# Sign of the float64 weights: from a ScalarE pass over one byte to a VectorE operation on the high word

## Chip, cores and metric

One core of a Trainium2 chip runs the whole program. The metric is the device time of that core in microseconds, as the median of several executions; a profiled execution is one more, with a span from its first to its last instruction.

## What is computed

Attention in which every query keeps its 32 best keys, over 8 batches x 8 heads x 576 positions x 64 dimensions, followed by a two-layer feed-forward block with an ELU between the layers, on 4608 tokens of width 512 and a hidden width of 2048:

```python
scores = scale * np.matmul(q, k.transpose(0, 1, 3, 2))
kth = np.partition(scores, -top_k, axis=-1)[..., -top_k:-top_k + 1]
scores = np.where(scores >= kth, scores, -1000000000.0)
scores = scores - np.max(scores, axis=-1, keepdims=True)
attn = np.exp(scores)
attn = attn / (np.sum(attn, axis=-1, keepdims=True) + 1e-09)
x = np.matmul(attn, v)          # (B,H,S,D) -> (B*S, H*D)
...
h = x @ w_in
g = np.where(h > 0.0, h, alpha * (np.exp(np.minimum(h, 0.0)) - 1.0))
out = g @ w_out
```

`q`, `k` and `v` arrive as float32. `w_in` and `w_out` arrive as float64, because the scaling of the random numbers promotes them; the kernel sees them as pairs of 32-bit words and turns them into float32 itself.

## The kernel before

**Steps.** The attention is cut into 144 steps. A step is 128 queries (a query tile, or the remainder rows) of a pair of heads. In a step TensorE computes scores for a step two ahead (L299) and ScalarE copies them out of PSUM (L307). VectorE finds the 32 best of each of 2 x 576 scores: it takes the 8 greatest (MAX8) and replaces them (MATCH_REPLACE8), four times and three times. GpSimd makes two small biases from the least and the greatest of the kept (L366, L368), ScalarE masks with a steep Prelu and takes the exponential (L369, L370), GpSimd normalises (L380 to L387), TensorE transposes (L406), ScalarE copies (L407), TensorE multiplies with `v` (L432), and ScalarE copies the result into `xT` (L459).

**Feed-forward pieces.** When all tiles of a block of tokens are in `xT`, its feed-forward work is cut into pieces: `hidden` (TensorE L504, ScalarE Relu twice and Exp, L514 to L519) and `project` (TensorE L529). `feed` puts pieces between attention work so that the total is spread evenly over the steps; a piece is held back until the weights that it needs count as decoded (`decoded`). The last operation of the activation function, a "gate" (L476), runs on VectorE: one operation with two tensors in, of 128x512 or 128x768.

**Who sets the order.** In the first eight steps (`n < tight`) a scheduler of the framework places the instructions of all engines, and `select_row` works row by row. From step 8 on the order is that of the program (`manual_schedule`), and `select` works on both rows at once. Each engine takes its instructions strictly in its order. Loads are issued on SyncE's queue.

**Weight decoding.** The weights come in 32 pieces of 128 x 512 numbers, 16 of `w_in` and 16 of `w_out`. `hook` is called after two of each row's passes and runs one `decode_piece` each time: four in one of the first eight steps, the last three in step 8. `load_weight` fetches a piece into a `raw` tile of 128 x 1024 words; seven such tiles take turns. In a `raw` tile the low and the high words alternate, so each is read with a stride of 8 bytes. `convert_first` works on three fields in place. ScalarE turns the low word into a small number that holds the lower mantissa bits (Copy, L174), turns one byte of the high word into a sign (Sign, L175, written as an 8-bit float into the top byte of the low word), and takes the scaled magnitude of the high word (Abs, L178). GpSimd clamps that magnitude (L179). Three pieces later `convert_last` shifts the high word left by three bits on VectorE (L186), and GpSimd adds the high and the low word as integers into the final tile, `w_in` or `w_out` (L187), which brings sign, exponent and mantissa together.

Of the kernel before, what the change touches and what calls it, by code (L numbers as in the profile page):

```python
# [8 lines left out]
AF = mybir.ActivationFunctionType  # L9
ALU = mybir.AluOpType  # L10
FP32 = mybir.dt.float32
U32 = mybir.dt.uint32
I32 = mybir.dt.int32
FP8 = mybir.dt.float8e4
PSUM = bass.MemoryType.PSUM

TOP_K = 32
# [64 lines left out]
def kernel(  # L82
# [9 lines left out]
    nc = tc.nc  # L92
# [9 lines left out]
    NF = dff // P  # L102
# [3 lines left out]
    scale = 1.0 / float(D) ** 0.5  # L106
# [33 lines left out]
    raw = {}  # L140

    def weight(i):
        per = dff // WN
        if i < NC * per:
            f, c = divmod(i, NC)
            src = moe_w_in[c * P : (c + 1) * P, 2 * f * WN : 2 * (f + 1) * WN]
            return src, w_in[:, c, f * WN : (f + 1) * WN]
        f = i - NC * per
        return moe_w_out[f * P : (f + 1) * P, :], w_out[:, f, :]

    def load_weight(i):
        t = rawpool.tile([P, 2 * WN], U32, tag="raw", name="raw")
        nc.sync.dma_start(t[:], weight(i)[0])
        raw[i] = t

    def parts(t):
        words = t[:].rearrange("p (n w) -> p n w", w=2)
        signs = t[:].bitcast(FP8).rearrange("p (n w) -> p n w", w=8)
        return words[:, :, 0], words[:, :, 1], signs[:, :, 3]

    def convert_first(i):

        lo, hi, sign = parts(raw[i])
        ef, mf = hi.bitcast(FP32), lo.bitcast(FP32)
        nc.scalar.activation(mf, lo, AF.Copy, scale=2.0**-35, bias=2.0**17)  # L174
        nc.scalar.activation(  # L175
            sign, ef, AF.Sign, scale=2.0**64, bias=1.0, saturate=False
        )
        nc.scalar.activation(ef, ef, AF.Abs, scale=2.0**-62)  # L178
        nc.gpsimd.tensor_scalar(  # L179
            ef, ef, (2.0 - 2.0**-3 - 2.0**-23) * 2.0**-46, 2.0**-77, ALU.min, ALU.max  # L180
        )

    def convert_last(i):
        t, dst = raw.pop(i), weight(i)[1]
        lo, hi, sign = parts(t)
        nc.vector.tensor_single_scalar(hi, hi, 3, ALU.logical_shift_left)  # L186
        nc.gpsimd.tensor_tensor(  # L187
            dst.bitcast(I32), hi.bitcast(I32), lo.bitcast(I32), ALU.add
        )

    decode = []
    decoded = [0]
# [10 lines left out]
            late["x"] = ctx.enter_context(tc.tile_pool(name="xt", bufs=2))  # L203

    def decode_piece(i):
        if i < 2 * NF:
            if i + 3 < 2 * NF:
                load_weight(i + 3)
            convert_first(i)
        if i > 2:  # L210
            convert_last(i - 3)
            decoded[0] = i - 2

    loaded, kqT, vT = {}, {}, {}

# [200 lines left out]
    def attend(g):  # L416
# [28 lines left out]
        while tiles:  # L445
            blk, lo, parts = tiles[0].block, tiles[0].cols.start, 0
            while tiles and tiles[0].block is blk:
                parts += 1
                hi = tiles.pop(0).cols.stop
            finish(blk, parts, g.hp, slice(lo, hi), ps[:, c0 : c0 + hi - lo])  # L450
            c0 += hi - lo
# [106 lines left out]
    for b in range(B):  # L558
# [12 lines left out]
        for qt in range(J + 1):  # L571
# [8 lines left out]
            t = Tile(b, qt, rows, blk, slice(c0, c0 + n))  # L580
# [6 lines left out]
        for qts in order:  # L587
# [3 lines left out]
            for qt in qts:  # L591
                n = len(steps)
# [54 lines left out]
    for hp in range(1, NHP):  # L647
        load_v(0, hp)
    decode += [lambda i=i: decode_piece(i) for i in range(2 * NF + 3)]
    at(0, start_qk, 0, 2)  # L650
    at(1, start_qk, 0, 3)
# [93 lines left out]
```

## Time and profile before

| quantity | value |
|---|---|
| median of 3 runs | 1667.17 us (1666.97 to 1669.18) |
| profiled execution | 1667.02 us, span 1665.2 us |
| TensorE matmul busy | 1592.8 us (96% of the span) |
| VectorE busy | 1495.8 us (90%) |
| ScalarE busy | 1165.1 us (70%) |
| GpSimd busy | 630.5 us (38%) |
| Copy on the low word, L174 | 32 x, 651 / 708 / 857 ns least, median, most |
| Sign into one byte, L175 | 32 x, 1327 / 1402 / 1589 ns |
| Abs on the high word, L178 | 32 x, 639 / 724 / 922 ns |
| clamp on GpSimd, L179 | 32 x, 638 / 658 / 923 ns |
| shift on VectorE, L186 | 32 x, 401 / 429 / 1281 ns |
| addition on GpSimd, L187 | 16 + 16 x, median 1038 and 1037 ns |
| gate on VectorE, L476 | 132 x, 660 / 692 / 1370 ns |

Durations of single instructions overlap: two MAX8 of some 0.75 us each are listed as 1.41 us together. What an instruction adds to a full engine is the time from its start to the start of the next. The decoding runs from 8.7 us (first Copy) to 148.6 us (start of the last addition); the rest of the span has none. A number in brackets at the end of a timeline row is the time for which the engine stood idle before it, with the instruction that ended the wait.

### The profile page before, as it was taken

What the parts mean: (1) busy time and instruction counts of PE and PEld (TensorE: products, weight loads), DVE (VectorE), ACT (ScalarE), POOL (GpSimd) and SP (SyncE); (2) the same over time, 40 slices, a digit from 0 to 9 for tenths busy, and PEclk for the clock granted to TensorE, in tenths of its full rate; (3) what the DMA queues carried; (4) which work ended last, traced back from release to release, by engine and by line L of the source; (5) the groups of instructions that cost most, each with busy time, mean ns of one, the idle gap of its engine ahead of it and who ended that gap; (6) DMA issues with size and microseconds to landing.
All of it is one profiled execution on the core that took longest, in us unless ns stands there. A gap on an engine that the chain in (4) does not pass through costs nothing.

```text
span 1665.2 us, 25986 instructions
## 1 busy us (share of the span) xinstructions
PE 1592.8 (96%) x8528; PEld 1031.5 (62%) x8528; DVE 1495.8 (90%) x3044; ACT 1165.1 (70%) x2377; POOL 630.5 (38%) x1719
## 2 busy tenths in 40 slices
PE   5589999999999999999999999999999999999999
PEld 3366677657574767656566676755557575755565
DVE  5887999999999999999999999999999999998500
ACT  6998777668686777678667685868758585857521
POOL 3775444333334334333334333333333343332200
PEclk9578999999999999999999999999999999999999
DMA  7540120001100110001100111001200100000000
GB/s 211 171 144 7 23 50 29 7 15 44 48 1 8 43 42 22 1 28 37 42 14 1 50 29 35 1 14 43 50 13 1 28 15 29 7 7 7 7 13 13
DMA packets 101126, 56.21 MB, mean 34 GB/s; under 512 B 84096, under 2 KB 92288, under 8 KB 100992
## 3 DMA queue, kind: packets, MB, share of 16 engines
q1 hardware_dynamic: 99792, 54.26, 11.7%
q8 instruction: 68, 1.11, 0.3%
q14 instruction: 66, 0.54, 0.1%
q10 hardware_dynamic: 1200, 0.30, 0.1%
HBM read 45.09 MB, written 9.44 MB: 33 GB/s over the span
## 4 chain that ended last, share of the span: by engine, by line
PE 65%; DVE 21%; ACT 9%; POOL 3%; issue 2%; SPq 0%; DMA 0%; ACTq 0%; POOLq 0%; DVEq 0%
PE ops L529 24%; PE hps L504 20%; DVE wk L346 9%; DVE m L353 8%; PE avps L432 7%; PE scps L299 6%; PE eps L406 5%; DVE m L341 3%; ACT sc L370 2%; ACT sc L369 1%; DVE gT L476 1%; ACT raw L175 1%; PE qkps L269 1%; ACT et L407 1%; POOL w_in L187 1%
## 5 line engine op out<-in xcount | busy, mean ns | idle before, releaser
L353 DVE MAX8 m<-wk 128x8 f32<-128x576 f32 x816 | 577.0, 750 | 0.0
L504 PE MATMUL hps<-xT,w_in 128*128 128x256 f32 (+2 forms) x2432 | 548.1, 374 | 12.5 <-ACT xT L459 12.3
L529 PE MATMUL ops<-w_out,gT 128*128 128x512 f32 x1152 | 522.8, 598 | 0.0
L504 PEld LDWEIGHTS hps<-xT,w_in 128*128 128x128 f32 x2432 | 406.5, 193 | 109.2 <-issue 23.8
L346 DVE MATCH_REPLACE8 wk<-m,wk 128x576 f32<-128x576 f32 x544 | 400.8, 746 | 0.0
L529 PEld LDWEIGHTS ops<-w_out,gT 128*128 128x128 f32 x1152 | 208.7, 190 | 233.0 <-issue 219.5
L380 POOL TENSOR_SCALAR dene<-den 128x2 f32<-128x2 f32 x144 | 35.9, 249 | 771.2 <-ACT sc L370 770.6
L369 ACT ACTIVATE sc<-sc,neg 128x576 f32<-128x576 f32 x288 | 226.8, 788 | 89.2 <-POOL neg L366 89.0
L370 ACT ACTIVATE sc<-sc,gap 128x576 f32<-128x576 f32 x288 | 224.1, 778 | 25.7 <-ACT sc L369 0.7
L387 POOL TENSOR_SCALAR sc<-sc,rec 128x576 f32<-128x576 f32 x288 | 221.0, 778 | 14.9
L307 ACT ACTIVATE sc<-scps 128x576 f32<-128x576 f32 x288 | 174.0, 659 | 73.3 <-PE scps L299 73.3
L299 PE MATMUL scps<-kqT 64*128 64x288 f32 (+1 forms) x1280 | 201.8, 440 | 21.2 <-ACT kqT L275 7.9
L407 ACT COPY et<-eps 128x512 f32<-128x512 f32 x288 | 166.8, 579 | 55.2 <-PE eps L406 55.0
L346 DVE MATCH_REPLACE8 wk<-m,sc 128x576 f32<-128x576 f32 x272 | 200.4, 746 | 0.0
L432 PE MATMUL avps<-et,vT 128*64 128x256 f32 (+2 forms) x2080 | 193.3, 326 | 4.8 <-ACT et L407 4.6
L406 PEld LDWEIGHTS eps<-ident,sc 128*128 128x128 f32 x1152 | 143.6, 144 | 83.8 <-issue 46.2
L476 DVE SCALAR_TENSOR_TENSOR gT<-n,gT 128x512 f32<-128x512 f32 (+1 forms) x132 | 100.2, 759 | 102.0 <-ACT n L519 101.9
L341 DVE MAX8 m<-sc 128x8 f32<-128x576 f32 x272 | 191.8, 748 | 0.0
L406 PE MATMUL eps<-ident,sc 128*128 128x128 f32 x1152 | 175.7, 278 | 15.4 <-POOL sc L387 13.0
L432 PEld LDWEIGHTS avps<-et,vT 128*64 128x64 f32 x2080 | 122.6, 141 | 79.1 <-issue 22.8
L299 PEld LDWEIGHTS scps<-kqT 64*128 64x128 f32 (+1 forms) x1280 | 108.1, 181 | 91.9 <-issue 44.2
L514 ACT ACTIVATE n<-hps 128x512 f32<-128x512 f32 (+1 forms) x156 | 88.0, 564 | 71.4 <-PE hps L504 67.5
(47 smaller groups left out, 1170.2 us busy)
## 6 DMA issues: line engine op xcount, KB each, us to landing
kin<-in_k_dram SPq DMA_DIRECT2D x64, 128.0 KB, 2.8
raw<-in_moe_w_in_dram SPq DMA_DIRECT2D x16, 512.0 KB, 5.4
vT<-in_v_dram SPq DMA_DIRECT2D x64, 128.0 KB, 2.3
raw<-in_moe_w_out_dram SPq DMA_DIRECT2D x16, 512.0 KB, 3.9
out_dram<-osb SPq DMA_DIRECT2D x32, 256.0 KB, 2.3
qin<-in_q_dram SPq DMA_DIRECT2D x62, 128.0 KB, 2.8
kin<-in_k_dram SPq DMA_DIRECT2D x32, 32.0 KB, 2.4
vT<-in_v_dram SPq DMA_DIRECT2D x64, 16.0 KB, 2.2
```

The costliest lines, as they stand in the source:

```text
L299: nc.tensor.matmul(wide[i][rows, half, 0:HS], kq[part, q0 : q0 + u.t.ql], kq[part, k0 : k0 + HS], start=True, stop=True,)
L341: nc.vector.max(found[i], cur[i])
L346: nc.vector.match_replace(wk[i], found[i], cur[i], TAKEN)
L353: nc.vector.max(found[i], cur[i])
L369: nc.scalar.activation(sc, sc, AF.Prelu, bias=neg[:], alpha=STEEP)
L370: nc.scalar.activation(sc, sc, AF.Exp, bias=gap[:], accum_out=u.den[:, i : i + 1])
L387: nc.gpsimd.tensor_scalar(u.sc[:, i, :], u.sc[:, i, :], rec[:, i : i + 1], 1.0, ALU.mult, ALU.mult)
L406: nc.tensor.transpose(ps[:, c * P : (c + 1) * P], sc[:, c0 : c0 + P], ident[:])
L407: nc.scalar.copy(g.et[:, chunks, u.at, :], ps[:, 0 : n * P].rearrange("p (c q) -> p c q", c=n),)
L432: nc.tensor.matmul(ps[i * D : (i + 1) * D, cols], vt[:, 2 * J + i if c == J else i * J + c, :], w, start=(c == 0), stop=(c == J),)
L504: nc.tensor.matmul(blk.h[:, f % bank, :], w_in[:, i, f * P : (f + 1) * P], blk.xT[:, i, 0:n_tok], start=(i == 0), stop=(i == NC - 1),)
L529: nc.tensor.matmul(blk.o[:], blk.gT[f // NG][:, f % NG, s * P : (s + 1) * P], w_out[:, f, :], start=(f == 0), stop=(f == NF - 1),)
```

## The change

The sign is no longer made by ScalarE. Abs writes the magnitude of the high word straight into the final tile, with another scale, and goes ahead of Copy. The clamp on GpSimd and the shift on VectorE work on the final tile in place. A new VectorE operation takes the sign bit of the untouched high word (AND with the top bit) and joins it (XOR) to the shifted magnitude. GpSimd's addition then adds the low word to the final tile. The four parts of a piece are issued in four successive calls of `decode_piece`: Abs and Copy at once, the clamp one call later, shift and sign two calls later, the addition three calls later. The number of calls, the number of loads and the count in `decoded` are as before.

```diff
@@ def parts(t):
         words = t[:].rearrange("p (n w) -> p n w", w=2)
-        signs = t[:].bitcast(FP8).rearrange("p (n w) -> p n w", w=8)
-        return words[:, :, 0], words[:, :, 1], signs[:, :, 3]
+        return words[:, :, 0], words[:, :, 1]
@@ def convert_first(i):
-        lo, hi, sign = parts(raw[i])
-        ef, mf = hi.bitcast(FP32), lo.bitcast(FP32)
-        nc.scalar.activation(mf, lo, AF.Copy, scale=2.0**-35, bias=2.0**17)
-        nc.scalar.activation(
-            sign, ef, AF.Sign, scale=2.0**64, bias=1.0, saturate=False
-        )
-        nc.scalar.activation(ef, ef, AF.Abs, scale=2.0**-62)
-        nc.gpsimd.tensor_scalar(
-            ef, ef, (2.0 - 2.0**-3 - 2.0**-23) * 2.0**-46, 2.0**-77, ALU.min, ALU.max
+        lo, hi = parts(raw[i])
+        nc.scalar.activation(weight(i)[1], hi.bitcast(FP32), AF.Abs, scale=2.0**-66)
+        nc.scalar.activation(lo.bitcast(FP32), lo, AF.Copy, scale=2.0**-35, bias=2.0**17)
+
+    def convert_second(i):
+        w = weight(i)[1]
+        nc.gpsimd.tensor_scalar(
+            w, w, (2.0 - 2.0**-3 - 2.0**-23) * 2.0**-50, 2.0**-81, ALU.min, ALU.max
         )
+
+    def convert_third(i):
+        w = weight(i)[1].bitcast(U32)
+        nc.vector.tensor_single_scalar(w, w, 3, ALU.logical_shift_left)
+        nc.vector.scalar_tensor_tensor(
+            out=w, in0=parts(raw[i])[1], scalar=1 << 31, in1=w,
+            op0=ALU.bitwise_and, op1=ALU.bitwise_xor,
+        )
@@ def convert_last(i):
-        t, dst = raw.pop(i), weight(i)[1]
-        lo, hi, sign = parts(t)
-        nc.vector.tensor_single_scalar(hi, hi, 3, ALU.logical_shift_left)
-        nc.gpsimd.tensor_tensor(
-            dst.bitcast(I32), hi.bitcast(I32), lo.bitcast(I32), ALU.add
-        )
+        w, t = weight(i)[1].bitcast(I32), raw.pop(i)
+        nc.gpsimd.tensor_tensor(w, w, parts(t)[0].bitcast(I32), ALU.add)
@@ def decode_piece(i):
-        if i < 2 * NF:
-            if i + 3 < 2 * NF:
-                load_weight(i + 3)
-            convert_first(i)
-        if i > 2:
-            convert_last(i - 3)
-            decoded[0] = i - 2
+        stages = (convert_first, convert_second, convert_third, convert_last)
+        if i + 3 < 2 * NF:
+            load_weight(i + 3)
+        for ago, stage in enumerate(stages):
+            if 0 <= i - ago < 2 * NF:
+                stage(i - ago)
+        decoded[0] = max(0, i - 2)
```

More of the change, by code (lines that the diff above doesn't have):

```diff
@@ L13 @@
 I32 = mybir.dt.int32
-FP8 = mybir.dt.float8e4
 PSUM = bass.MemoryType.PSUM
```

## The prediction

> **What bounds the kernel now.** I read the chain that ended last first, then the engines by stage, then the order of work on ScalarE and VectorE inside the first stage, since the edit touches nothing after it (the last shift of a weight piece, L186, starts at 148.1 us). The chain by engine, from the page:
>
> ```profile
> PE 65%; DVE 21%; ACT 9%; POOL 3%; issue 2%; SPq 0%; DMA 0%; ACTq 0%; POOLq 0%; DVEq 0%
> ```
>
> ACT's 9% (some 150 us) matters here. The stages, columns as PE, PEld, DVE, ACT, POOL busy us with counts, clock granted to PE, DMA share, GB/s:
>
> ```profile
> 52.00:67.00 15.00, 9.90 (x40) 7.20 (x41) 12.06 (x26) 14.30 (x26) 11.21 (x20) 0.50 0.62 177
> ...
> 127.00:142.00 15.00, 10.88 (x65) 8.18 (x64) 5.02 (x11) 15.00 (x28) 7.84 (x13) 0.74 0.01 2
> 150.00:200.00 50.00, 49.47 (x371) 36.26 (x370) 50.00 (x103) 38.34 (x81) 23.45 (x65) 1.00 0.07 18
> ...
> 400.00:800.00 400.00, 392.29 (x2075) 251.49 (x2072) 400.00 (x816) 291.79 (x610) 152.72 (x442) 1.00 0.10 27
> ```
>
> While weights are decoded ScalarE is full and VectorE has gaps; from 150 us on VectorE is full without a gap and TensorE nearly so. So what the edit is worth is how much earlier or later VectorE, and TensorE with it, enters that full stretch. One step (one pair of attention rows) of ScalarE's timeline:
>
> ```profile
> 51.80 0.24 ACT L459 COPY xT<-avps 128x128 f32<-128x128 f32 x1
> ...
> 59.78 1.28 ACT L174 ACTIVATE raw<-raw 128x512 f32<-128x512 uint32 x2
> 60.90 2.53 ACT L175 ACTIVATE raw<-raw 128x512 fp8e4<-128x512 f32 x2
> 63.12 1.29 ACT L178 ACTIVATE raw<-raw 128x512 f32<-128x512 f32 x2
> 64.28 0.80 ACT L369 ACTIVATE sc<-sc,neg 128x576 f32<-128x576 f32 x1
> ...
> 66.76 0.30 ACT L459 COPY xT<-avps 128x128 f32<-128x128 f32 x1
> ```
>
> The step takes 66.76 - 51.80 = 14.96 us. Instructions overlap, so I take a price from start to next start: Copy 0.56, Sign 1.11, Abs 0.58 us. With four pieces in a step, decoding is 4 x 2.25 = 9.0 us of ScalarE and everything else 6.0. VectorE waits behind it, through GpSimd:
>
> ```profile
> DVE raw L186 <- POOL raw L179: 38.3, 19, 12.2
> POOL raw L179 <- ACT raw L178: 33.7, 9, 9.8
> ```
>
> VectorE's own prices, and the point at which it enters the full stretch:
>
> ```profile
> 16.89 1.41 DVE L318 MAX8 m<-sc 128x8 f32<-128x576 f32 x2
> ...
> 26.54 0.74 DVE L318 MAX8 m<-sc 128x8 f32<-128x576 f32 x1
> 27.20 0.41 DVE L186 TENSOR_SCALAR raw<-raw 128x512 uint32<-128x512 uint32 x1
> 27.52 0.08 DVE L322 MATCH_VALUE_LOAD wk<-m,sc 128x8 f32 x1
> ...
> 59.63 1.27 DVE L186 TENSOR_SCALAR raw<-raw 128x512 uint32<-128x512 uint32 x1
> ...
> 107.26 0.68 DVE L476 SCALAR_TENSOR_TENSOR gT<-n,gT 128x512 f32<-128x512 f32 x1
> 107.85 0.09 DVE L322 MATCH_VALUE_LOAD wk<-m,wk 128x8 f32 x1
> ...
> 138.53 0.69 DVE L476 SCALAR_TENSOR_TENSOR gT<-n,gT 128x512 f32<-128x512 f32 x1 [3.42 <-ACT n L519]
> ```
>
> One step's selection is 26.54 - 16.89 = 9.65 us; a shift 27.52 - 27.20 = 0.32; a two-tensor operation of 128x512 is 107.85 - 107.26 = 0.59. Behind the gate at 138.53 the full stretch starts, with the first replacement of step 8 at 139.2. The one long shift (59.63, 1.27 us instead of 0.41) stands beside this row of GpSimd:
>
> ```profile
> 59.58 1.04 POOL L187 TENSOR_TENSOR w_in<-raw 128x512 int32<-128x512 int32 x1
> ```
>
> It began 0.05 us after GpSimd's addition and ended after it: it was held up until GpSimd was through.
>
> **The change, part by part.** *Sign on ScalarE goes:* 32 x 1.11 = 35.5 us of ScalarE, and a step there falls to 14.96 - 4 x 1.11 = 10.5 us. ScalarE no longer bounds the stage. *Abs writes the final tile and stands ahead of Copy:* same two operations, 0.58 and 0.56; no cost, and GpSimd's clamp can start 0.56 us sooner. *The clamp* works in place on the final tile: 32 as before, 0.64 to 0.65 us where nothing holds them. *The final addition* reads the final tile instead of the high words: two inputs as before, 1.04 us. GpSimd per step: four clamps and additions 6.8, a normalisation (L380 to L387) 3.5, masks 0.8, so about 11 us; it stays under VectorE's step. *The shift* now runs on the final tile: I keep 0.32. *The new operation* (sign bit of the high word, joined to the shifted magnitude) is not in the trace; the nearest row is L476, also two tensors in, 128x512 of 32 bits, 0.59 us. Its high words lie 8 bytes apart, but the old shift ran at 0.32 on words just so spaced, so I add nothing. The lower bound is a shift's 0.32, the upper a GpSimd addition's 1.04 (also two inputs, spaced); by nearness 0.59. Over 32 it is 18.9 us of VectorE. *Loads:* weight loads number the same; in SyncE's order some of the second batch's key and query loads move past a weight load or two, some earlier, some later. ScalarE waited for weights only 5.2 us, twice, both before 13.1 us, so this costs nothing unless a load is over a step late. *TensorE's order* changes a little: feed-forward matmuls of the first block go out in one run of 41 instead of several; no operation is added.
>
> *The sum on VectorE, up to that first replacement of step 8.* Before: first MAX8 at 16.89; 8 steps x 9.65 = 77.2; two MAX8 of step 8, 1.33; 27 shifts x 0.32 = 8.6; four gates x 0.59 = 2.4; waits 38.3 - 12.19 - 3.90 (the two before the first MAX8) = 22.2 on GpSimd and 6.0 on ScalarE's Exp; and hold-ups: of 13 shifts that did not wait (up to 148.1), two took 0.87 and two together 0.43 more than usual, 2.2 in all. That gives 136.8, so 2.4 us of small items is left to reach 139.2; I keep it.
>
> After: the first MAX8 moves from 16.89 to about 15.2. ScalarE's score copies (15.67) stand behind Sign and Abs of the second piece, which landed at 13.04; without Sign they can go at 14.2. VectorE first has that piece's pair to do: 13.04 + 0.58 + 0.65 + 0.32 + 0.59 = 15.2. Then 77.2 + 1.33 + 2.4 + 2.4, and 28 pairs (by the program's order) x 0.91 = 25.5: 124.0, plus hold-ups c and waits i. Behind the mark stand two pairs (1.8) instead of three shifts (1.0): +0.9. So the shift at the end of the stage is d = 124.0 + 0.9 - 139.2 + c + i = -14.3 + c + i.
>
> *c.* 30 pairs are 60 operations that can collide with GpSimd. The unwaited shifts lost 2.2/13 = 0.167 us each; that gives 10.0, which I take. Lower bound: the 108 gates of 128x512 average 708 ns against a median of 692 over all gates, 0.02 each, 1.2 in all. Upper bound: GpSimd is busy 11.2 of 15 us (52 to 67), and an operation that always meets it at random waits half of some 0.85 us: 0.75 x 0.43 = 0.32, 19 in all. *i.* The new shift waits on GpSimd's clamp, with MAX8 of the selection queued behind it, and for those wait the mask (L366), ScalarE's exponentials, GpSimd's scaling and TensorE's transposes. Half of the 3.00 us wait before 40.97 should stay, since it follows from step 0's mask and normalisation, and a quarter of the 6.0 us for Exp: 3.0. Bounds 0 and 10. So d = -14.3 + 10.0 + 3.0 = **-1.3 us**. TensorE can follow: between 95 and 141 us it waits 1.61, 3.11, 1.19 and 2.86, all behind ScalarE or GpSimd, 8.8 together. The profiled execution is 1667.0 us (span 1665.2, 1.8 around it), the median 1667.2; so **1665.9 us**.
>
> The Trainium skill speaks against the change here: "SBUF — State Buffer", section "Who interferes with whom", says that a VectorE instruction with two SBUF inputs, like one in a two-port mode, locks out a GpSimd instruction that reads SBUF for its whole length, and the other way round. The row at 59.63 shows this for the shift, and the longest gate (1.37 us, where its two forms average 0.71 and 0.99) fits it for two inputs. Were every one of the 60 held for half of a 1.04 us addition, c would be 31 and the time about 1687; the gates' mean shows that most do not collide.
>
> **The rivals.** *Full relief.* VectorE and GpSimd fall into step and rarely collide: c = 60 x 0.045 (between the gates' 0.02 and the 0.07 by which the mean shift, 492 ns, exceeds a free one) = 2.7, i = 1, d = -10.6, of which TensorE's 8.8 us of waits can follow: 1658.4. For it: 19 of 32 shifts ran in waits and cost 0.43. Against it: those were free because VectorE was starved; now it is not. *The port decides: slower.* With c at 19.4 and i = 3, d = +8.1 and the time is 1675.3: a step of VectorE is then 9.65 + 4 x 0.91 + 8 x 0.32 = 15.9 us, longer than ScalarE's 14.96 was. It decides from c + i = 14.3 on, and is over 0.2% from 17.6 on, at 0.24 us per operation. For it: GpSimd's share of 0.75. Against it: 0.167 measured. *TensorE binds anyway.* It is full from 136.6 us; if it does not reach that point sooner, nothing comes of VectorE's gain: 1667.2. Against it: its 8.8 us of waits.
>
> **How the numbers follow.** About 0.2%, 3.3 us, is what a measurement of this kernel can tell from no change. The sum as chosen, c + i from 9 to 17.6 (1662 to 1670.5): 0.42, of which 0.30 lies within 0.2% and 0.12 is faster. Full relief 0.24, the port 0.30, TensorE binds 0.04. So faster 0.36, within 0.34, slower 0.30. The range, 1656 to 1676, reaches to both outer cases.
>
> **What would show it.** Right: ScalarE with gaps from 50 to 140 us and a step of 14 to 15.5 us on it; the new operation near 0.59 from start to start, some stretched to over 1.1 us beside GpSimd additions; VectorE's waits after 17 us under 8 us; first replacement of step 8 at 135 to 139 us. Wrong: the new operation at 1 us or more even alone, a step above 16 us, or the step-8 mark early by more than 5 us with the end unmoved.

## The result: slower, and the profile after

The changed kernel takes 1686.95 us (median of 4, 1685.83 to 1687.32) beside 1668.18 us (1666.97 to 1669.41) of the kernel before: ratio 1.011, 95% interval 1.0094 to 1.0126. The profiled execution has a span of 1685.5 us, 20.3 more than before. The forecast of 1665.9 and its range, 1656 to 1676, both miss it.

The chain of waits by engine, after:

```profile
PE 74%; DVE 11%; ACT 7%; POOL 4%; issue 2%; DMA 0%; ACTq 0%; POOLq 0%
```

The part of VectorE fell from 21% to 11%, that of TensorE rose from 65% to 74%. The same four windows as in the prediction (PE, PEld, DVE, ACT, POOL busy us with counts, granted clock, DMA share, GB/s):

```profile
52.00:67.00 15.00, 9.75 (x37) 6.25 (x37) 12.96 (x26) 7.96 (x17) 13.26 (x17) 0.50 0.44 140
127.00:142.00 15.00, 7.81 (x46) 6.60 (x45) 12.60 (x25) 9.14 (x18) 10.26 (x17) 0.73 0.19 67
150.00:200.00 50.00, 43.76 (x277) 30.59 (x278) 43.81 (x90) 29.23 (x60) 26.00 (x55) 0.85 0.02 6
400.00:800.00 400.00, 391.48 (x2093) 254.75 (x2093) 400.00 (x818) 291.23 (x607) 151.85 (x440) 1.00 0.10 27
```

The last row is that of before within a few tenths of a per cent: nothing changed behind the first stage. In the first row ScalarE is relieved as forecast (14.30 to 7.96 us), but VectorE isn't full either (12.96 of 15); the engine nearest to full is now GpSimd, 13.26 of 15 instead of 11.21. The third row is the surprise: from 150 to 200 us, where VectorE had been full, it has 6.2 us of gaps and TensorE the same.

The copies into `xT` on ScalarE (L459, in the changed kernel L458) come once in a step here and mark where it ends. Their starts, and in brackets the time since the one before, from ScalarE's timelines of six kernels (the four variants are described below):

| copy | before | after | no new operation | no Sign | MAX8 in its place | back + clamp moved |
|---|---|---|---|---|---|---|
| 1 | 51.80 | 48.89 | 46.88 | 47.46 | 47.00 | 44.03 |
| 2 | 66.76 (15.0) | 65.03 (16.1) | 61.83 (15.0) | 60.44 (13.0) | 61.41 (14.4) | 54.56 (10.5) |
| 3 | 81.75 (15.0) | 84.27 (19.2) | 76.88 (15.1) | 73.77 (13.3) | 79.24 (17.8) | 72.91 (18.4) |
| 4 | 96.71 (15.0) | 101.45 (17.2) | 90.11 (13.2) | 87.02 (13.3) | 96.50 (17.3) | 89.09 (16.2) |
| 5 | 112.43 (15.7) | 126.58 (25.1) | 103.24 (13.1) | 100.53 (13.5) | 118.74 (22.2) | 112.48 (23.4) |
| 6 | 128.07 (15.6) | 145.26 (18.7) | 117.81 (14.6) | 115.71 (15.2) | 136.71 (18.0) | 128.82 (16.3) |
| 7 | 145.22 (17.2) | 163.02 (17.8) | 131.63 (13.8) | 130.62 (14.9) | 153.33 (16.6) | 144.32 (15.5) |
| 8 | 160.17 (15.0) | 182.58 (19.6) | 146.09 (14.5) | 147.31 (16.7) | 171.90 (18.6) | 162.24 (17.9) |

The changed kernel is 2.9 us ahead at the first copy, 1.7 at the second, 2.5 behind at the third and 22.4 behind at the eighth. Steps of 16 to 25 us took the place of steps of 15; one of them, the fifth, brings 9.4 us of the loss.

What TensorE, GpSimd and VectorE waited for between 17 and 165 us (total, times, longest), after:

```profile
PE eps L405 <- POOL sc L386: 46.1, 7, 11.0
POOL w_out L174 <- ACT w_out L169: 22.7, 13, 4.5
...
POOL w_in L174 <- ACT w_in L169: 9.6, 5, 6.3
DVE m L317 <- POOL gap L367: 8.5, 2, 6.1
DVE w_in L180 <- POOL w_in L174: 8.3, 4, 5.4
...
DVE m L340 <- POOL gap L367: 1.7, 1, 1.7
DVE w_out L180 <- POOL w_out L174: 0.4, 1, 0.4
```

The first of these rows, before:

```profile
PE eps L406 <- POOL sc L387: 13.0, 5, 3.4
```

TensorE's transposes wait for the normalised scores, the last work of GpSimd in a step. And VectorE waits not only for clamps: twice it cannot start MAX8 of the next selection because GpSimd has not yet read the old maxima for its small bias (`gap`). GpSimd itself stood at its clamps for 22.7 + 9.6 = 32.3 us, waiting for ScalarE's Abs (before, 23.8).

The chain of work that ended last, cut out between 17 and 165 us, shows the change of engine: before, its pieces add up to some 66 us on ScalarE and 31 on GpSimd, after, to 17 on ScalarE and 57 on GpSimd.

Where GpSimd's time goes is seen in its timeline in a stretch without a gap, after (start, us, instruction):

```profile
44.10 1.29 POOL L188 TENSOR_TENSOR w_in<-w_in,raw 128x512 int32<-128x512 int32 x1
45.47 0.94 POOL L174 TENSOR_SCALAR w_in<-w_in 128x512 f32<-128x512 f32 x1
46.49 1.53 POOL L188 TENSOR_TENSOR w_in<-w_in,raw 128x512 int32<-128x512 int32 x1
48.10 0.94 POOL L174 TENSOR_SCALAR w_in<-w_in 128x512 f32<-128x512 f32 x1
49.12 1.29 POOL L188 TENSOR_TENSOR w_in<-w_in,raw 128x512 int32<-128x512 int32 x1
50.50 0.67 POOL L174 TENSOR_SCALAR w_in<-w_in 128x512 f32<-128x512 f32 x1
51.25 0.23 POOL L379 TENSOR_SCALAR dene<-den 128x2 f32<-128x2 f32 x1
...
53.60 1.84 POOL L188 TENSOR_TENSOR w_in<-w_in,raw 128x512 int32<-128x512 int32 x1
55.43 0.74 POOL L386 TENSOR_SCALAR sc<-sc,rec 128x576 f32<-128x576 f32 x1
```

Six operations of decoding run almost without a gap ahead of the normalisation, and one addition stands inside it. An addition takes 1.29 us where it took 1.04, and more beside VectorE's two-input operation: the one at 53.60 takes 1.84 us, and VectorE's new operation starts at 53.63. The transposes that wait for the last row shown and its like start at 56.23 after 5.81 us of idle TensorE.

The fifth step, the worst, in four rows of four timelines, after:

```profile
103.52 10.90 PE L503 MATMUL hps<-xT,w_in 128*128 128x128 f32 x82
```

```profile
108.20 0.60 ACT L513 ACTIVATE n<-hps 128x512 f32<-128x512 f32 x1 [4.22 <-PE hps L503]
```

```profile
110.44 0.61 POOL L174 TENSOR_SCALAR w_out<-w_out 128x512 f32<-128x512 f32 x1 [4.54 <-ACT w_out L169]
```

```profile
111.53 0.76 DVE L317 MAX8 m<-sc 128x8 f32<-128x576 f32 x1 [6.09 <-POOL gap L367]
```

The first block's feed-forward goes out as one run of 82 matmuls. ScalarE takes its instructions in order and stands at the Relu of that run for 4.22 us; behind it stands the Abs of the next weight piece, for which GpSimd's clamp waits; behind the clamp stand GpSimd's two small biases, and for the second of these VectorE waits 6.09 us. Before, the same work went out in runs of 18, 18, 40 and 6 spread over the step, and ScalarE did not wait there.

### The profile page after: what moved, and what is told of

It reads as the page before. It is cut to its first block, busy times and chain, and to the rows that moved or that the text cites. A ratio compares the mean times of both kernels' runs of the same rounds, so it can differ in the third digit from the quotient of the medians.

```text
span 1685.5 us, 25971 instructions
## 1 busy us (share of the span) xinstructions
PE 1601.0 (95%) x8528; PEld 1036.0 (61%) x8528; DVE 1521.7 (90%) x3076; ACT 1133.3 (67%) x2345; POOL 642.2 (38%) x1719
## 4 chain that ended last, share of the span: by engine, by line
PE 74%; DVE 11%; ACT 7%; POOL 4%; issue 2%; DMA 0%; ACTq 0%; POOLq 0%
PE ops L528 27%; PE hps L503 23%; PE avps L431 9%; PE scps L298 8%; PE eps L405 6%; DVE wk L345 5%; DVE m L352 4%; ACT sc L369 1%; DVE m L340 1%; ACT sc L368 1%; PE qkps L268 1%; ACT et L406 1%; POOL sc L386 1%; PE scps L405 1%; POOL w_in L188 1%
## 5 line engine op out<-in xcount | busy, mean ns | idle before, releaser
L386 POOL TENSOR_SCALAR sc<-sc,rec 128x576 f32<-128x576 f32 x288 | 220.9, 777 | 14.9
L405 PE MATMUL eps<-ident,sc 128*128 128x128 f32 x1152 | 178.1, 281 | 48.0 <-POOL sc L386 46.1
L298 PE MATMUL scps<-kqT 64*128 64x288 f32 (+1 forms) x1280 | 207.8, 444 | 10.8 <-ACT et L406 6.2
```

What stands on the lines that cost most here:

```text
L298: nc.tensor.matmul(wide[i][rows, half, 0:HS], kq[part, q0 : q0 + u.t.ql], kq[part, k0 : k0 + HS], start=True, stop=True,)
L386: nc.gpsimd.tensor_scalar(u.sc[:, i, :], u.sc[:, i, :], rec[:, i : i + 1], 1.0, ALU.mult, ALU.mult)
L405: nc.tensor.transpose(ps[:, c * P : (c + 1) * P], sc[:, c0 : c0 + P], ident[:])
```

## The experiments

In diffs, lines are those of the changed kernel unless the kernel before is named. Times are medians; the kernel before ran beside each at 1666.6 to 1667.9 us, so a difference of a microsecond between two experiments says nothing. The versions without Sign, without the new operation, or with MAX8 in its place leave the signs out.

**What the relief is worth.** The kernel before without Sign:

```diff
-        nc.scalar.activation(
-            sign, ef, AF.Sign, scale=2.0**64, bias=1.0, saturate=False
-        )
```

> The kernel before without the Sign pass on ScalarE (the signs of the weights are left out); nothing is added on VectorE. Theory 1 (port: VectorE and GpSimd lock each other out, so GpSimd's normalisation is late and TensorE waits): no new two-input work on VectorE, so no loss; ScalarE's relief of 35 us shows as far as TensorE's 8.8 us of waits allow, 1656 to 1662. Theory 2 (order: once ScalarE is relieved, the order that the framework's scheduler picks makes the engines wait for each other): no gain or a loss, 1667 to 1690. Theory 3 (VectorE's 19 us of new work): 1656 to 1662, as theory 1.

Measured: 1654.02 us, ratio 0.9921 (0.9892 to 0.995). The relief is worth 13.1 us, more than the 8.8 of TensorE's waits that the prediction let it reach, and more than any of the three theories allowed. And the changed kernel without the new operation:

```diff
-        nc.vector.scalar_tensor_tensor(
-            out=w, in0=parts(raw[i])[1], scalar=1 << 31, in1=w,
-            op0=ALU.bitwise_and, op1=ALU.bitwise_xor,
-        )
```

> The changed kernel without the new VectorE operation (the signs are left out); clamp, shift and addition stay as changed. Theory 3 (VectorE's 19 us): the whole loss goes, 1664 to 1669. Theory 1 (port): about half of the hold-ups go with one of two colliding operations, while the slower addition (1.29 us) stays: 1672 to 1680. Theory 2 (order): 1680 to 1690.

Measured: 1656.50 us, 0.9936 (0.9913 to 0.9958). This too is faster than all three theories said. So the stages, the final tile in place of the raw one and the slower addition cost some 2.5 us by the medians while VectorE has room (the two intervals overlap); all else comes with the new operation and the order that the scheduler makes with it, 30.5 us for 18.9 us of VectorE.

**Its time, or its second input?** In place of the new operation VectorE does a MAX8 over 512 words of the final tile, one input, nearly the same length. The order of instructions on every engine stays that of the changed kernel.

```diff
-        nc.vector.scalar_tensor_tensor(
-            out=w, in0=parts(raw[i])[1], scalar=1 << 31, in1=w,
-            op0=ALU.bitwise_and, op1=ALU.bitwise_xor,
-        )
+        junk = small.tile([P, 8], FP32, tag="junk", name="junk")
+        nc.vector.max(junk[:], w.bitcast(FP32))
```

> The changed kernel with the new operation replaced by a MAX8 over the same 512 words of the final tile (one tensor in, about as long on VectorE; the signs are left out). The order of instructions on every engine stays that of the changed kernel, to the last one. If the second tensor input matters (VectorE and GpSimd lock each other out): most of what taking the operation out gave back stays away only by VectorE's time, so 1670 to 1678. If it is VectorE's time and the order that goes with it: 1684 to 1688, as the changed kernel.

Measured: 1676.79 us, 1.006 (1.0043 to 1.0077). The groups of VectorE in this kernel (count, busy us, mean ns), and then the new operation's in the changed kernel:

```profile
L182 DVE MAX8 junk<-w_in 128x8 f32<-128x512 f32 x16 | 10.9, 681 | 0.1
L182 DVE MAX8 junk<-w_out 128x8 f32<-128x512 f32 x16 | 10.9, 680 | 0.1
```

```profile
L181 DVE SCALAR_TENSOR_TENSOR w_out<-raw,w_out 128x512 uint32<-128x512 uint32 x16 | 13.3, 829 | 0.1
L181 DVE SCALAR_TENSOR_TENSOR w_in<-raw,w_in 128x512 uint32<-128x512 uint32 x16 | 12.8, 803 | 0.1
```

MAX8 was never held up (695 ns at most); the two-input operation takes 667 to 684 ns free and 0.80 to 0.83 us in the mean, up to 1.75 us beside an addition. With the same order, the new operation costs 1686.95 - 1676.79 = 10.1 us more than MAX8. This is called the price of the second input below, but MAX8 differs in one more thing: it writes 8 words of a row and not 512, and no run separates the two. The Trainium skill ("SBUF — State Buffer", "Who interferes with whom") says that two SBUF inputs on VectorE contend with a GpSimd instruction that reads SBUF, and that at most one input does not, outside the two-port modes. The new operation and MAX8 agree with it; the one-input shift was held up in both kernels (0.53 and 0.56 us in the mean after, 0.50 and 0.54 with MAX8, over a free 0.41), which the page allows only for an operation in such a mode; no row names the mode. The other 20.3 us, from 1656.5 to 1676.8, come with 32 x 0.60 us (from its start to the next start) = 19.2 us of VectorE and with the order that the scheduler makes for it.

**How much is the order?** Four kernels take the first eight steps in program order too:

```diff
+    ctx.enter_context(tc.manual_schedule(engines=engines))
...
-        if n == tight:
-            ctx.enter_context(tc.manual_schedule(engines=engines))
```

> The kernel before, with the first eight steps in the order of the program too (manual schedule from step 0). All theories: slower than with the scheduler, 1670 to 1720; it is the base for the next run.

> The changed kernel, with the first eight steps in the order of the program too. Theory 2 (order picked by the scheduler): within 6 us of the kernel before in program order. Theories 1 and 3: 12 to 25 us slower than the kernel before in program order.

> Program order in the first eight steps, the new operation taken out (the signs are left out); every other instruction stands where it stood in the changed kernel in program order (1685.9). If the 30 us that taking it out gave with the scheduler were a matter of another order picked by the scheduler: 1665 to 1675. If they are the operation's own doing: 1650 to 1660.

> Program order in the first eight steps, with the MAX8 in place of the new operation (the signs are left out). Lock-out: clearly under 1685.9, by 6 to 14 us. VectorE's time alone: within 3 us of 1685.9.

Measured: the kernel before 1738.34 us (1.0426, 1.0396 to 1.0457), the changed one 1685.91 (1.0112, 1.0083 to 1.0141), without the new operation 1675.99 (1.0048, 1.0032 to 1.0064), with MAX8 in its place 1682.46 (1.0086, 1.0066 to 1.0106). In this order the change makes the kernel 52 us faster, which fits neither theory, and the kernel before is slower than its forecast. The scheduler is worth 71 us to the kernel before and nothing to the changed one. The operation's time costs 6.5 us here, the second input 3.4 (two intervals that overlap), together 9.9 instead of 30.5. So the price of the new operation hangs on the order around it. How much of the 30.5 us is the order's doing does not follow: in program order TensorE waits 51.3 us for the normalised scores (17 to 170 us) even without the new operation, in the scheduler's order 18.8, so there is more waiting behind which its time can hide.

**The order, changed by hand.** Mask and normalisation of the first eight steps get a raised priority in the scheduler, in the changed kernel and, as a control, in the kernel before:

```diff
-                    normalise(prev)
+                    with tc.high_priority():
+                        normalise(prev)
...
-                mask(cur, i)
+                with tc.high_priority():
+                    mask(cur, i)
```

> The changed kernel, with the mask and the normalisation of the first eight steps (GpSimd's and ScalarE's part of them) given precedence over the decoding in the scheduler; the same instructions in another order. If a good part of the loss is order (GpSimd held by clamps and additions while the normalisation that TensorE waits for stands behind them): 1660 to 1679, with TensorE's wait for the normalised scores (46 us up to 170 us) under 30. If it is VectorE's time and the lock-out alone: 1683 to 1690.

> The kernel before, with a raised priority for the mask and the normalisation of the first 8 steps, the edit that took 7.6 us off the changed kernel. Theory (the order puts decoding ahead of the attention's chain only in the changed kernel, where VectorE's piece of decoding has grown): little to gain here, 1664 to 1668. Rival (the order costs both kernels alike, and the gain has nothing to do with the change): about 1660.

Measured: the changed kernel 1679.38 us (1.0075, 1.0058 to 1.0092), 7.6 less; the kernel before 1676.51 (1.0055, 1.004 to 1.007), 9.1 more. So the same instructions in another order are worth 7.6 us one way in one kernel and 9.1 us the other way in the other, which neither forecast for the kernel before allowed. Why it helps the changed kernel is not shown: the forecast wanted TensorE's wait for the normalised scores under 30 us, and it is still 43.0 (46.1 without the priority). What went are VectorE's waits for `gap`, 8.5 + 1.7 us, of which none is left.

**GpSimd's addition.** First its inputs are exchanged, then (second diff) the new operation writes its result back over the raw high words, so that the addition again reads two strided inputs and writes to another tile:

```diff
-        nc.gpsimd.tensor_tensor(w, w, parts(t)[0].bitcast(I32), ALU.add)
+        nc.gpsimd.tensor_tensor(w, parts(t)[0].bitcast(I32), w, ALU.add)
```

> The changed kernel with the two inputs of GpSimd's addition exchanged (low word first, final tile second). If the addition takes 1.29 us instead of 1.04 because of which input is spaced: back to about 1.04, and 2 to 8 us come back (1679 to 1685). If it is because it works in place, or because of two differently spaced inputs: 1.29 stays and so does the time.

```diff
-            out=w, in0=parts(raw[i])[1], scalar=1 << 31, in1=w,
+            out=parts(raw[i])[1], in0=parts(raw[i])[1], scalar=1 << 31, in1=w,
...
-        nc.gpsimd.tensor_tensor(w, w, parts(t)[0].bitcast(I32), ALU.add)
+        lo, hi = (x.bitcast(I32) for x in parts(t))
+        nc.gpsimd.tensor_tensor(w, hi, lo, ALU.add)
```

> The changed kernel, but the new operation writes its result back over the high words of the raw tile, and GpSimd adds high and low words into the final tile, as the kernel before did. Theory (the addition got 0.25 us slower because it works in place on one contiguous input, and GpSimd is late in this stage): the free addition is back at 1.04 instead of 1.29 us, 32 x 0.25 = 8 us of GpSimd, and since the matmuls of the attention wait for GpSimd, 3 to 8 us of it come off the time: 1679 to 1684. Rival (GpSimd's lateness comes from collisions and order, the addition's own length is hidden): addition at 1.04, the time within 2 us of the changed kernel's 1687. Second rival (the addition is slow for another reason): still 1.29.

> The result written back over the raw high words and the raised priority together. If the addition's length and the order are separate costs: 7.6 us less than the write-back alone, 1672 to 1676. If one covers the other: not under 1679.

One addition in the first kernel, one in the second, from GpSimd's timelines:

```profile
42.88 1.30 POOL L188 TENSOR_TENSOR w_in<-raw,w_in 128x512 int32<-128x512 int32 x1
```

```profile
42.34 1.04 POOL L189 TENSOR_TENSOR w_in<-raw 128x512 int32<-128x512 int32 x1
```

Measured: exchanged 1685.73 us (1.0105, 1.0085 to 1.0126), still 1.29 to 1.30 per addition where nothing holds it; written back 1681.73 (1.0098, 1.008 to 1.0115), with 1.04 where nothing holds it; written back with the raised priority 1673.81 (1.0037, 1.0024 to 1.005), 5.6 under the priority alone. On every engine the instructions stand in the changed kernel's order in both single edits. Which input comes first is not the reason; the form is, one contiguous input that is also the output. Whether the contiguous input or the working in place makes it slow is not separated. The write-back alone gives 5.2 us by the medians, which its interval does not separate from the changed kernel's; the pair with the priority does separate, and gives nearly the same. It is less than the 7.6 us by which the 32 additions got shorter in the mean (1438 and 1347 ns to 1154).

**The clamp off GpSimd.** The clamp on VectorE, in the changed kernel, with the write-back, and with write-back and priority:

```diff
-        nc.gpsimd.tensor_scalar(
+        nc.vector.tensor_scalar(
             w, w, (2.0 - 2.0**-3 - 2.0**-23) * 2.0**-50, 2.0**-81, ALU.min, ALU.max
```

> The changed kernel with the clamp on VectorE (one tensor in, about 0.33 us) instead of GpSimd (0.61 us). It takes some 20 us from GpSimd and gives some 10 to VectorE. If GpSimd's queue is what delays TensorE: 1665 to 1680. If VectorE is: 1690 to 1700.

> The write-back over the raw high words (1681.7 us) and the clamp of each piece on VectorE instead of GpSimd (which alone took 10.8 us off the changed kernel). If both give back GpSimd's time and add up: 1681.7 - 10.8 = 1670.9. If they relieve the same lateness of GpSimd, and one is enough: about 1676, as the clamp's move alone.

> All three together: result written back, clamp on VectorE, raised priority for mask and normalisation in the first 8 steps. If all add up: 1673.8 - 10.8 = 1663.0, which would be under the kernel before (1667.4). If VectorE is now the engine that is late in the stage (32 more operations on it): not under 1671.

Measured: 1676.18 us (1.0058, 1.0038 to 1.0079), 1671.94 (1.0026, 1.0017 to 1.0036) and 1672.04 (1.0027, 1.0016 to 1.0037). VectorE gets 32 operations more, and the kernel is 10.8 us faster for it: it was GpSimd, with decoding ahead of masks and normalisation in its queue, that was late. In the chain from 17 to 165 us its pieces fall from some 57 us to 32. (The scheduler's order changes with this edit too.) With the write-back it adds up (9.8 more), but the priority on top gives nothing. The windows of the second kernel:

```profile
43.00:65.00 22.00, 10.40 (x53) 6.99 (x53) 22.00 (x45) 17.00 (x34) 12.27 (x21) 0.66 0.64 182
65.00:95.00 30.00, 24.15 (x101) 17.14 (x102) 30.00 (x62) 17.21 (x34) 15.90 (x25) 0.52 0.49 160
95.00:140.00 45.00, 28.93 (x171) 23.14 (x170) 45.00 (x92) 29.45 (x58) 24.60 (x38) 0.68 0.25 82
```

VectorE is now full without a gap from 43 to 140 us, so the priority finds none to close, and the version ends 4.4 us behind the kernel before. That VectorE's load now bounds the stage is read from these rows and not shown: none of the longer pieces of the chain that ended last, between 17 and 165 us, is VectorE's.

**A mixture, and another relief.** Every second piece in the old way, every second in the new one; the same with the raised priority; and the kernel before with the low word shifted on VectorE in place of ScalarE's Copy:

```diff
-            if 0 <= i - ago < 2 * NF:
-                stage(i - ago)
+            j = i - ago
+            if 0 <= j < 2 * NF:
+                stage = (new if j % 2 == 1 else old)[ago]
+                if stage:
+                    stage(j)
```

> Every second weight piece is decoded the old way (Sign on ScalarE), every second the new way. If the two ways trade one full engine for another (ScalarE against VectorE with GpSimd): both engines come under 13 us a step, and it beats both, 1655 to 1664. If the new way's loss is a matter of the order or of GpSimd: between the two, 1668 to 1680.

> Every second piece in the old way and every second in the new one, with the raised priority for mask and normalisation. If the gain of the priority (7.6 us on the changed kernel) is in proportion to the new operations in the stage, half of it: 1670.5 - 3.8 = 1666.7. If it comes in full: 1663, which would be under the kernel before. If it hangs on the particular order the scheduler finds: anywhere from 1663 to 1675.

```diff
-        nc.scalar.activation(mf, lo, AF.Copy, scale=2.0**-35, bias=2.0**17)
+        nc.vector.tensor_single_scalar(lo, lo, 29, ALU.logical_shift_right)
```

> The kernel before with the low word shifted right by 29 on VectorE (one tensor in, 0.32 us) instead of scaled by Copy on ScalarE (0.56 us); Sign stays on ScalarE; the low bits are cut off instead of rounded. It takes 18 us from ScalarE, the full engine, and gives VectorE 10 us of operations without a second tensor. If one-tensor work on VectorE is cheap while ScalarE is full: 1657 to 1664. If any VectorE work in this stage costs what it lasts or more: 1666 to 1680.

Measured: 1670.53 us (1.0021, 1.0012 to 1.003), 1672.13 (1.0031, 1.0019 to 1.0043), and 1671.11 (1.0024, 1.0014 to 1.0034). Half of the change costs 3.9 us by the medians, a fifth of the whole: the loss grows faster than the number of new operations. The priority does not help here; its effect hangs on the order that the scheduler finds. The one-input shift, 32 times 563 ns in the mean in place of ScalarE's 729, still loses 4.5. No run that computes the whole result is faster than the kernel before.

**The long run of matmuls.** In all kernels that follow the scheduler and have an extra operation of VectorE on every piece, the longest run of feed-forward matmuls between 60 and 165 us is 52 to 82, and the fifth step takes 19.8 to 25.1 us; in the kernel before, in the two without Sign or without the new operation and in the two mixtures it is 38 to 40 matmuls and the fifth step 13.1 to 17.7. (The kernel before with the raised priority has runs of 24 at most and a fifth step of 18.7, so the run is not the only way to a long one; and in program order runs of at most 24 stand beside fifth steps of 17.4 to 26.3.) One of the long runs, with MAX8 in place; without the new operation the longest is 40 matmuls of 4.73 us, from 100.09:

```profile
97.70 9.42 PE L501 MATMUL hps<-xT,w_in 128*128 128x128 f32 x82
```

Between these two kernels the fifth step differs by 9.1 us, the others by -0.5 to 4.1 (four operations of 0.60 are 2.4). No experiment changed this run alone, so that it costs some 7 us is read from the traces and not tested.

## Why the prediction was wrong, step by step

- **Right: what ScalarE gives.** It has gaps from 50 to 140 us and the relief reaches the end. It is worth 13.1 us and not the 8.8 to which the prediction held it: those were TensorE's waits after 95 us alone, while from 17 us on the old trace has 13.0 for the normalised scores and 12.3 for the copies into `xT`.
- **Right: the new operation and the hold-ups on VectorE.** 0.59 to 0.60 us from start to start where free, as the gate's row said. By the means, shifts and new operations lost 16 x (0.119 + 0.151 + 0.129 + 0.155) = 8.9 us over their free 0.41 and 0.67, against c = 10.0. The first MAX8 came at 15.62 (forecast 15.2).
- **Wrong: i, the waits.** Taken at 3.0 with bounds 0 and 10, measured 8.5 + 8.3 + 1.7 + 0.4 = 18.9, where under 8 was to show that the prediction is right; steps above 16 us, a sign of its being wrong, came too. The first replacement of step 8 came at 151.16 and not at 124.0 + 13.0 = 137.0: 14.2 us later, against 15.9 us of waits more than forecast and 1.1 of hold-ups less. The step took the waits to follow from what GpSimd waits for. It did not see that GpSimd would be late by its own work, nor that its clamps would stand still for 32.3 us behind a ScalarE that waits for TensorE and for GpSimd itself.
- **Wrong: GpSimd's cost of nothing.** The prediction left the addition at 1.04 us because it has two inputs as before. It takes 1.29 in its new form: 5 to 6 us of the time. And it counted what VectorE loses by collisions, but not what GpSimd does: additions 1.44 and 1.35 in the mean over a free 1.29, clamps 0.70 and 0.64 over a free 0.61, and the small operations behind them. "It stays under VectorE's step" compared 11 us with 14 and so missed that the last of GpSimd's work in a step, the normalisation, stands behind the decoding in its queue. The second input costs 10.1 us in all, in the same order, and not only the c of VectorE.
- **Wrong: "TensorE's order changes a little; no operation is added".** Order alone, with no operation added, is worth 7.6 us in the changed kernel and 9.1 in the kernel before, when the priority is raised. The operation's time costs 20.3 us in the scheduler's order and 6.5 in program order, and the longest run, 82 matmuls in the trace, stands in the step that lost 9.4 us. The prediction named that run and priced it at zero.
- **Wrong: the mark on VectorE as the measure of the end.** VectorE's mark moved by 12.0 us, the span by 20.3. TensorE's first long run of `project` matmuls moved from 141.11 to 162.90, 21.8 us, and with it the end. TensorE had to wait for GpSimd 46.1 us, and its granted clock was lower in the stage, 0.67 instead of 0.82 from 100 to 150 us. The two rows, before and after:

```profile
100.00:150.00 50.00, 42.41 (x236) 30.58 (x235) 33.61 (x72) 45.92 (x82) 31.58 (x50) 0.82 0.19 63
```

```profile
100.00:150.00 50.00, 33.79 (x202) 27.66 (x198) 39.45 (x75) 31.25 (x62) 30.31 (x45) 0.67 0.31 103
```

- **Small: loads cost nothing.** Not quite: ScalarE waited for `w_out` pieces 1.9 us, twice, after 130 us, since a raw tile comes free only with the late addition. The chain that ended last runs through these two loads for 3.17 and 3.47 us; before, through one for 3.03.
- **The rivals.** "The port decides: slower" had the right sign and part of the mechanism, but at 1675.3 it counted only VectorE's side. The rule of the Trainium skill ("SBUF — State Buffer", "Who interferes with whom") taken at its word, "about 1687", hit the number by luck, not for its reason: it charged 31 us of hold-ups to VectorE, where 8.9 arose; the rest came from GpSimd and the order.

The account in the scheduler's order: -13.1 for the relief, +2.5 for stages and form of the addition, +20.3 for the new operation's time with the order that goes with it, +10.1 for its second input; sum +19.8, measured 18.8 between the medians. The terms are differences of one row of runs, so they must add up; the 1.0 is the kernel before, which ran 1.1 us slower beside the changed kernel than beside the experiments that start the row. Of the loss, 5 to 6 us go when the addition has its old form, 7.6 when the priority changes the order, 10.8 when the clamp leaves GpSimd; together they give 14.9 and not their sum.

Open: how the 20.3 us divide between VectorE's own time and the order. Program order says 6.5 and 13.8, but it has a different order throughout.

## What to carry to other kernels

Price an operation that is moved between engines with the order in mind: where a scheduler makes the order, compare the two instruction lists of every engine, and treat a helper's work that has come ahead of a chain's last step as a cost, a long run as a possible one. Look at the third engine: here the relieved and the loaded one did not decide alone, but GpSimd, two thirds busy (97.16 of 148 us from 17 to 165), because the chain's last work stood behind decoding in its queue. And a form of an instruction (in place, contiguous beside strided) is part of its price, so a row for the same operation in another form is a bound and not the value.

## What the hardware showed that was not expected

- GpSimd's integer addition of 128x512 takes 1.04 us with two inputs 8 bytes apart and a separate contiguous output, and 1.29 us in place with one contiguous and one strided input, whichever of the inputs comes first.
- A one-input MAX8 of 128x512 beside GpSimd's decoding was not lengthened at all (680 ns in the mean of 32), a two-input operation of the same free length was, by a fifth, and the one-input shift by about a third (0.53 and 0.56 us over 0.41). With MAX8 in place of the two-input operation, in the same order, the kernel is 10.1 us faster.
- Taking 35.5 us of work off the fullest engine of a stage gained 13.1 us, and adding 19 us to one with gaps lost 30.5.
